# Block attention and an ELU feed-forward on one core: the second product of the last six blocks also taken as seven products of halves, transposed, with a list schedule for the work around it

## The chip, the core and the metric

The kernel runs on one core of a Trainium2 chip. Its engines work side by side, each through its own list of instructions in order: TensorE (PE in the profile, its weight loads PEld) multiplies matrices, VectorE (DVE), ScalarE (ACT) and GpSimd (POOL) do elementwise work, and SyncE (SP) issues the transfers between the chip's memory (HBM) and the core's own memory (SBUF). Matrix products land in PSUM, eight banks of 128 x 512 floats. Engines wait for each other by semaphores. The metric is the time of one execution on the device in microseconds (us).

## The reference

```python
# q, k, v: (8, 8, 576, 64) = batch, heads, tokens, head_dim
q_c, k_c, v_c = [t.reshape(B, H, 9, 64, D) for t in (q, k, v)]     # chunks of 64 tokens
scores = matmul(q_c, k_c^T) / sqrt(64);  attn = softmax(scores)    # within a chunk
x = matmul(attn, v_c) -> (4608 tokens, 512)
h = x @ w_in                                  # w_in (512, 2048)
g = where(h > 0, h, exp(min(h, 0)) - 1)
out = g @ w_out                               # w_out (2048, 512), float32
```

## The kernel before

The 4608 tokens are nine blocks of 512. x is kept transposed (features down the partitions, tokens along), so the first product gives h transposed, 128 hidden features by 512 tokens at a time (16 such rows, f = 0 to 15), and g, transposed in the same way, is the stationary operand of the second product, whose result stands in four PSUM banks o0 to o3 of 128 tokens each. Every operand of the two large products is kept as two numbers, a rounded high part and the rest (hi and lo, `ghi` and `glo`), and every product of 128x128 by 128x512 is three matmuls, hi hi + hi lo + lo hi (`three`, L400 on). ACT makes the high part, DVE or POOL the rest.

The first three blocks do this directly; the weights come in and are split in the first of them. Beside it runs the attention of a later tile of 128 tokens (`Later`): two stream transposes of q and k on DVE, 32 small matmuls for the scores, maximum and subtraction on DVE, one exponential over 128x512 on ACT, sums and normalisation on DVE, a transpose, four small transfers that swap quarters (`turned<-unturned`), and the product with v. The third block is written out by `THIRD_BLOCK`, a table of steps per f.

The last six blocks go two at a time (three rounds, `s`), and there the first product alone is made of seven products of halves (`Pair`, `PRODUCTS`): x of the two blocks and w_in are cut into 2x2 parts, sums of parts of w_in (S1 to S4) are made once and lie in HBM (`a_dram`), sums of parts of x (T1 to T4) are made by `prepare` per round, and seven products (`p1` to `p7`, six matmuls each) with kept copies and additions (`c`, `d`) give four rows of h. One pair g = 42 matmuls. The second product of the first block of the round runs in between (`Q`: three matmuls, 24 a pair), the second product of the second block stands behind all eight pairs (`KEPT`: 192 matmuls). The orders are tables written by hand (`PAIR`, `KEPT`); each letter is a step, issued on whatever engines it uses. SP loads the next operands of w_in in pieces of 256 KB in rows of 1 KB (`wi_hi<-a_dram`) and the low parts of w_out (`wo_lo<-lo_dram`, 512 KB in rows of 4 KB). Outputs of 128 tokens x 512 leave PSUM through one copy and one transfer of 256 KB in rows of 2 KB (`copy_out`).

Of the kernel before, what the change touches and what calls it, by code (L numbers as in the profile page):

```python
# [20 lines left out]
def kernel(  # L21
# [26 lines left out]
    P = 128  # L48
# [59 lines left out]

    def load_unit(u: int):
# [10 lines left out]
        if f >= 0:  # L120
            nc.sync.dma_start(
                out=st[:, len(parts)].rearrange("p a b t -> p (a b t)"),
                in_=w_out[f * P:(f + 1) * P, :],
            )
            parts.append([w.rearrange("p (a b) -> p a b", a=4) for w in w_out_slices(f)])
# [20 lines left out]
    def merge_units():  # L146
# [6 lines left out]
        for u in range(NU):  # L153
# [17 lines left out]
            for i, (hi, _) in enumerate(parts):  # L171
                nc.scalar.copy(out=hi, in_=y[:, i].bitcast(F32))
                merged.append((parts[i], y[:, i].bitcast(F32)))
# [22 lines left out]
    def load_heads(src, name: str, n0: int, pool):  # L196
        dst = pool.tile([P, H, D], F32, name=name)
# [5 lines left out]

    def load_tokens(n0: int, qk):
# [3 lines left out]
        U = 4  # L208
        for i, src in enumerate((q, k)):
            for j in range(2):  # L210
                for half in range(2):
                    w0 = i * NK * U * D + (1 - half) * Q
                    for p0, b, s0, n in pieces_of(n0, U):
                        p0 += j * D + half * Q
                        nc.sync.dma_start(
                            out=qk[p0:p0 + n // U, w0:w0 + NK * U * D].rearrange(
                                "p (h w) -> p h w", h=NK),
                            in_=src[b, j::2, s0:s0 + n, :].rearrange("h (t u) d -> t h (u d)", u=U),
                        )
# [97 lines left out]
    class Later:  # L317
# [5 lines left out]
        def load_qk(self):  # L323
            self.st = place_of_tokens(self.n)
            self.qk = load_tokens(self.n * P, self.st)
# [33 lines left out]
        def turn_a(self):  # L359
# [5 lines left out]
                op=ALU.mult)  # L365
            nc.vector.transpose(
                out=turned.rearrange("p e (j h) t -> p j h e t", j=2),
                in_=self.scores.rearrange("p j h (e k) -> p j h e k", e=2))
            nc.scalar.copy(out=unturned, in_=turned)
            for c in range(2):  # L370
# [57 lines left out]

    def elu(h, engine=nc.vector):

        e = gp.tile([P, TB], F32, name="e")
# [7 lines left out]
        ghi = gp.tile([P, TB], F32R, name="ghi")  # L439
        nc.scalar.copy(out=ghi, in_=e)  # L440
        yield
        glo = gp.tile([P, TB], F32R, name="glo")
# [3 lines left out]
    def copy_out(o, n0: int, src, on_vector: bool):  # L446

        (nc.vector.tensor_copy if on_vector else nc.scalar.copy)(out=o, in_=src)
        nc.sync.dma_start(out=out[n0:n0 + P, :], in_=o)

    def store(blk: int, o_ps):
        for tt in range(NTT):
            o = io.tile([P, DM], F32, name="q_sb" if tt % 2 else "k_sb")
            copy_out(o, blk * TB + tt * P, o_ps[tt], False)
# [609 lines left out]
```

## Time and profile before

| | |
|---|---|
| median of 3 runs | 840.24 us (840.18 to 840.9) |
| profiled execution, first to last instruction | 840.2 us |
| PE busy, granted clock | 826.3 us (98%), 0.995 of full |
| DVE, ACT, POOL busy | 501.6, 480.4, 179.0 us (60%, 57%, 21%) |
| transfers | 164.09 MB, 195 GB/s over the span |

The page gives one time for the profiled execution, its span; it stands 0.04 us below the median of the runs, so nothing of size lies around it. A row of the profile names the line of the kernel, the engine, the operation, output<-inputs, the shape, and a count; then the busy time and the mean time of one in ns. A matmul of 128x512 is listed with some 390 ns, but the next one starts before it ends, so the pace is read from chains of them. "Idle before" is time in which the engine had nothing to do, with what ended it. DMA share is the mean busy share of the 16 transfer engines.

### The profile page before, as it was taken

How to read it: one execution, taken by the hardware profiler on the slowest of the kernel's cores; microseconds unless marked ns; L12 is line 12 of the kernel's file. 1: busy time of each engine (PE TensorE's matmuls, PEld its weight loads, DVE VectorE, ACT ScalarE, POOL GpSimd, SP SyncE). 2: the span in 40 equal slices, each digit the busy share in tenths (PEclk: the TensorE clock that was granted, in tenths of full speed). 3: DMA queues.
4: the chain of work that ended last, by engine and by line, in shares of the span. 5: the costliest groups of instructions: out<-in, count | busy, mean ns of one | idle time of the engine just before them, and what ended most of it. 6: DMA issues, size and time to landing. Idle time of an engine off the chain costs nothing.

```text
span 840.2 us, 15685 instructions
## 1 busy us (share of the span) xinstructions
PE 826.3 (98%) x5949; PEld 677.0 (81%) x5949; DVE 501.6 (60%) x719; ACT 480.4 (57%) x825; POOL 179.0 (21%) x149
## 2 busy tenths in 40 slices
PE   7899999999999999999999999999999999999998
PEld 6788888887888888888888888778888888888886
DVE  4999997666775679565666746566555333233411
ACT  5999875444554547656666436655664355555521
POOL 0000014445312221111114521111126211111120
PEclk8999999999999999999999999999999999999999
DMA  9875754865787777698888656779844365545331
GB/s 240 263 228 187 247 181 152 271 205 183 232 234 218 207 193 218 191 258 239 241 240 242 191 149 200 199 233 257 238 146 138 111 198 160 164 144 163 101 101 50
DMA packets 178794, 164.09 MB, mean 195 GB/s; under 512 B 65568, under 2 KB 161312, under 8 KB 178720
## 3 DMA queue, kind: packets, MB, share of 16 engines
q1 hardware_dynamic: 178720, 163.10, 66.0%
q8 instruction: 47, 0.77, 0.4%
q14 instruction: 27, 0.22, 0.1%
HBM read 131.07 MB, written 28.31 MB: 190 GB/s over the span
## 4 chain that ended last, share of the span: by engine, by line
PE 92%; ACT 2%; DVE 2%; DMA 2%; SPq 1%; issue 1%; DVEq 0%; ACTq 0%
PE o L408 45%; PE h L408 40%; PE ps_a L235 2%; PE ps_a L243 2%; PE h L425 1%; DMA turned<-unturned 1%; SPq L199 1%; DMA k_sb<-in_k_dram 1%; PE ps_a L257 1%; PE ps_a L302 1%; SPq L373 0%; ACT st L135 0%; ACT a L280 0%; DVE e L435 0%; ACT e L433 0%
## 5 line engine op out<-in xcount | busy, mean ns | idle before, releaser
L408 PE MATMUL o<-wo_hi,ghi 128*128 128x512 f32 x416 | 163.8, 394 | 0.1
L408 PE MATMUL o<-wo_hi,glo 128*128 128x512 f32 x416 | 162.2, 390 | 0.0
L408 PE MATMUL o<-wo_lo,ghi 128*128 128x512 f32 x416 | 162.0, 390 | 0.0
L590 POOL TENSOR_TENSOR glo<-e,ghi 128x512 fp32r<-128x512 f32 x46 | 59.5, 1293 | 318.4 <-ACT ghi L588 318.4
L408 PE MATMUL h<-xhi,wi_hi 128*128 128x512 f32 x324 | 108.1, 394 | 0.0
L408 PE MATMUL h<-xlo,wi_hi 128*128 128x512 f32 x324 | 106.7, 389 | 0.0
L408 PE MATMUL o<-wo_hi,wo_lo 128*128 128x512 f32 x320 | 99.2, 389 | 0.0
L408 PEld LDWEIGHTS o<-wo_hi,ghi 128*128 128x128 f32 x416 | 78.1, 188 | 17.4 <-ACT ghi L440 0.5
L408 PEld LDWEIGHTS o<-wo_hi,glo 128*128 128x128 f32 x416 | 78.1, 188 | 16.7 <-DVE glo L443 0.4
L408 PEld LDWEIGHTS o<-wo_lo,ghi 128*128 128x128 f32 x416 | 78.1, 188 | 15.8
L629 ACT COPY kept<-h 128x512 f32<-128x512 f32 x72 | 42.2, 586 | 62.1 <-PE h L408 62.0
L408 PE MATMUL h<-wi_lo,wi_hi 128*128 128x512 f32 x288 | 75.0, 396 | 0.0
L408 PE MATMUL h<-wo_lo,wi_hi 128*128 128x512 f32 x288 | 72.9, 389 | 0.0
L408 PEld LDWEIGHTS h<-xhi,wi_hi 128*128 128x128 f32 x324 | 60.8, 188 | 12.9
L408 PEld LDWEIGHTS h<-xlo,wi_hi 128*128 128x128 f32 x324 | 60.8, 188 | 12.2
L408 PEld LDWEIGHTS o<-wo_hi,wo_lo 128*128 128x128 f32 x320 | 60.1, 188 | 12.5
L408 PE MATMUL h<-xhi,wi_lo 128*128 128x512 f32 x180 | 70.2, 390 | 0.0
L583 DVE SCALAR_TENSOR_TENSOR g_kept<-e,g_kept 128x512 f32<-128x512 f32 x48 | 33.2, 692 | 61.4 <-ACT e L580 61.4
L633 DVE TENSOR_TENSOR g_kept<-h,kept 128x512 f32<-128x512 f32 x48 | 33.1, 690 | 51.8 <-ACT kept L629 27.2
L408 PEld LDWEIGHTS h<-wo_lo,wi_hi 128*128 128x128 f32 x288 | 54.1, 188 | 11.2
L580 ACT ACTIVATE e<-e 128x512 f32<-128x512 f32 x96 | 60.7, 632 | 3.1
L408 PE MATMUL o<-wo_lo 128*128 128x512 f32 x160 | 62.2, 389 | 0.0
(114 smaller groups left out, 1330.3 us busy)
## 6 DMA issues: line engine op xcount, KB each, us to landing
wi_hi<-a_dram SPq DMA_DIRECT2D x168, 256.0 KB, 3.9
wo_lo<-lo_dram SPq DMA_DIRECT2D x52, 512.0 KB, 4.5
kept<-in_q_dram SPq DMA_DIRECT2D x100, 128.0 KB, 3.5
kept<-in_k_dram SPq DMA_DIRECT2D x100, 128.0 KB, 3.9
v_sb<-in_v_dram SPq DMA_DIRECT2D x32, 256.0 KB, 6.2
st<-in_moe_w_in_dram SPq DMA_DIRECT2D x16, 512.0 KB, 4.0
st<-in_moe_w_out_dram SPq DMA_DIRECT2D x16, 512.0 KB, 5.2
a_dram<-kept SPq DMA_DIRECT2D x16, 512.0 KB, 4.1
```

What stands on the lines that cost most here:

```text
L199: nc.sync.dma_start(out=dst[p0:p0 + n], in_=src[b, :, s0:s0 + n, :].rearrange("h s d -> s h d"))
L235: nc.tensor.matmul(scores[halves[c], j, hp, :], lhsT=qT[halves[j], hp, halves[c]], rhs=kT[halves[j], hp, halves[c]], start=True, stop=True,)
L243: nc.tensor.matmul(x_ps[halves[j], c, hp, :], lhsT=v_sb[halves[c], 2 * hp + j, :], rhs=aT[halves[c], :, j * NK + hp], start=True, stop=True,)
L257: nc.tensor.transpose(out=both[:, i, hp * P:(hp + 1) * P], in_=src[:, 2 * hp:2 * hp + 2, :], identity=ident,)
L302: nc.tensor.matmul(turned_ps[half, h, :], lhsT=a[half, h, :], rhs=ident[half, half], start=True, stop=True,)
L408: nc.tensor.matmul(ps, lhsT=a, rhs=b, start=start, stop=stop, skip_group_check=onto)
L425: nc.tensor.matmul(h, lhsT=w[:, kt, :], rhs=x[:, kt, :], start=i == 0, stop=i == len(terms) - 1)
L580: nc.scalar.activation(out=e, in_=e, func=AF.Exp, scale=-1.0)
L583: nc.vector.scalar_tensor_tensor(out=to, in0=e, scalar=-1.0, in1=c, op0=ALU.add, op1=ALU.max)
L590: engine.tensor_tensor(out=lo, in0=e, in1=hi.bitcast(F32), op=ALU.subtract)
L629: nc.scalar.copy(out=c21 if i == 4 else self.kept[i - 1], in_=x_ps)
L633: nc.vector.tensor_tensor(out=to, in0=y_ps, in1=self.kept[kept], op=ALU.add)
```

## The change

The first three blocks stay as they were, except that the 512 columns of w_out are stored in another order (`in_order`; outputs undo it on the way out), and that between the steps of the third block POOL, ACT and DVE form sums of parts of w_out (`combine_w_out`, four of eight; SP writes them to `w_dram`, and parts of w_out to `hi_dram`). The other four are made at the start of the last six blocks (`add_sums`).

In the last six blocks each round has two phases. In the first, the seven products of the first product are made for all eight g's (336 matmuls), with g of the 2x2 parts left in SBUF (`g_first`, `g_more`). In the second, the second product is made of seven products too (`SECOND`), now with w_out as the stationary operand and g as the moving one, so that the result is transposed: 7 x 8 x 6 = 336 matmuls. For it the parts of g are first subtracted and added among themselves (24 operations a round, line 1254), every one of 56 operands is split into hi and lo, and the results are added (DVE), turned back by stream transposes of DVE and sent in pieces of 64 columns (`add_out`, rows of 256 bytes). All stationary operands of both phases come through one ring of four places of 512 KB (`load_entry`), 56 loads a round.

The order is no longer a table. Every step is a job of a `Plan` with an engine, a cost in ns and the keys that it reads and writes; PE's order is fixed by the numbers given, and `Plan.order` sets jobs on ACT, DVE, POOL and SP by how soon PE needs them. Some elementwise jobs may go to DVE or POOL (`EITHER`). The exponential of a tile is made by head there: eight ACT instructions of 128x64 with the maximum as bias and the sum as a by-product, in place of a subtraction and a sum on DVE.

```diff
-    class Pair:
-    ...
-        def product(self, i: int):
-            to = y_ps if i in (2, 5, 3) else x_ps
-            (ah, al), (bh, bl) = a_operand(i), b_operand(PRODUCTS[i][1])
-            for k in range(2):
-                three(to, ah[:, k, :], al[:, k, :], bh[:, k, :], bl[:, k, :],
-                      i in (1, 2, 5) and k == 0, k == 1, onto=i not in (1, 2, 5))
-            if self.g + 1 < NS * NG:
-                load_a(self.g + 1, i)
-    PAIR = (
-        "m p1 c1 4 E Q 4 z p2 d1 Q p6 c2 h 1 Q Q 1 p5 1 q k 1 Q l p7 c3 d2 Q Q 2 p4 c4 2 Q 3 p3 d3 "
-        "3 3 3 s v x V"
-    )
+    FIRST = (1, 2, 6, 5, 7, 3, 4)
+    SECOND = (1, 2, 4, 6, 5, 7, 3)
+    PAIRS = NG // 2
+    ENTRIES = 2 * 7 * PAIRS
+    def load_entry(e: int):
+        slot, (phase, e) = ring_slot(e), divmod(e % ENTRIES, 7 * PAIRS)
+        if not phase:
+            d, o = divmod(e, 7)
+            parts = [(slot, a_dram[AOPS.index(PRODUCTS[FIRST[o]][0]), :, 2 * d:2 * d + 2])]
+        ...
+        for to, of in parts:
+            nc.sync.dma_start(out=to.bitcast(F32), in_=of)
+    def product_second(i: int, j: int, e: int, s: int, to):
+        slot = ring_slot(e)[:, j % 2].rearrange("p l (i d) -> p l i d", i=2)
+        for c in range(2):
+            three(bank(to[c]), slot[:, 0, c], slot[:, 1, c], split_place(s, 0), split_place(s, 1),
+                  i in (1, 2, 4, 5) and j == 0, j == NG - 1, onto=i not in (1, 2, 4, 5))
     ...
+    def add_softmax(t: float, n: int, begun: bool = False):
+            ...
+            def exp_by_head():
+                later[n].z = sm.tile([P, 2, NK, 1], F32, name="z")
+                for j in range(2):
+                    for h in range(NK):
+                        nc.scalar.activation(
+                            out=later[n].scores[:, j, h, :], in_=later[n].scores[:, j, h, :],
+                            func=AF.Exp, scale=SCALE, bias=mx[0][:, j, h, :],
+                            accum_out=later[n].z[:, j, h, :])
+    def add_entry(t: float, e: int):
+        count = entry_jobs(e)
+        plan.add(t, "SP", dma(count, 1320), lambda: load_entry(e),
+                 [("sums", j) for j in summed(e)], [("ring", e % 4)])
+    def add_out(t: float, s: int, h: int, c: int, sources, keys, place, place_keys):
+        ...
+        for i in range(2):
+            plan.add(t + .01 * i, "DVE", (630, 716), turn_(i), [keys[i]], [place_keys[i]])
+        plan.add(t + .05, "SP", dma(4, 2300), send, list(place_keys), [])
```

How the change moves instructions shows in three places. On PE, ahead of the profile's 624 us mark in the kernel before (second product of the second block of a round; `wo_lo` on the right side of the arrow also names the places of g's split parts, which lie in a buffer of that name), before:

```order
L408 MATMUL o_6538<-wo_hi,wo_lo 128x512
L408 MATMUL o_6538<-wo_lo 128x512
L408 MATMUL o_6538<-wo_hi,wo_lo 128x512
L408 MATMUL o_6539<-wo_hi,wo_lo 128x512
L408 MATMUL o_6539<-wo_lo 128x512
L408 MATMUL o_6539<-wo_hi,wo_lo 128x512
```

and now, in the second phase of the last round (`split`, `ghi` and `glo` are the split parts of g, `ring` a place of the ring):

```order
L434 MATMUL h<-ghi,ring 128x512
L434 MATMUL h<-split,ring 128x512 x24
L434 MATMUL o_3717<-ghi,ring 128x512
L434 MATMUL o_3717<-glo,ring 128x512
L434 MATMUL o_3717<-ghi,ring 128x512
L434 MATMUL o_3731<-ghi,ring 128x512
```

What was four banks of 128 tokens, three matmuls each, for 16 f's is now two banks at a time, six matmuls a job, for eight j's and seven products; each job waits for one split part and, every second job, for a ring place.

On SP, in the first of the last six blocks, before (one pair; `kept` from q and k is the load of a tile's tokens):

```order
L373 DMA turned<-unturned 32x256 x4
L533 DMA wi_hi<-a_dram 128x2x256
L215 DMA kept<-in_q_dram 32x4x256 x4
L215 DMA kept<-in_k_dram 32x4x256 x4
L533 DMA wi_hi<-a_dram 128x2x256 x2
L549 DMA wo_lo<-lo_dram 128x1024
L533 DMA wi_hi<-a_dram 128x2x256
L199 DMA v_sb<-in_v_dram 128x8x64
```

and now at the start of the first phase of the first round:

```order
L1599 DMA out_dram<-g_first 128x512
L598 DMA w_dram<-g_more 128x4x256 x2
L1145 DMA ring<-a_dram 128x1024 x2
L598 DMA w_dram<-g_more 128x4x256 x2
L399 DMA turned<-unturned 32x256 x4
L1145 DMA ring<-a_dram 128x1024 x2
L227 DMA kept<-in_q_dram 32x4x256
L1145 DMA ring<-a_dram 128x1024
L227 DMA kept<-in_q_dram 32x4x256 x3
L227 DMA kept<-in_k_dram 32x4x256 x3
L1145 DMA ring<-a_dram 128x1024
```

Ring loads of 512 KB stand between the same loads of tokens and, in this first phase, between the writes of the sums of w_out.

On DVE, at the end of the program, before:

```order
L448 COPY kept<-o_6813 128x512
L448 COPY kept<-o_6815 128x512
L590 TENSOR_TENSOR wo_lo<-g_kept,wo_lo 128x512 x8
L448 COPY g_kept<-o_7654 128x512
L448 COPY g_kept<-o_7656 128x512
```

and now:

```order
L1500 TENSOR_TENSOR glo<-g_more,ghi 128x512
L1251 TENSOR_TENSOR spare<-h,spare 128x512
L1251 TENSOR_TENSOR kept<-h,kept 128x512
L1251 TENSOR_TENSOR spare<-h,spare 128x512
L1251 TENSOR_TENSOR kept<-h,kept 128x512
L1411 STREAM_TRANSPOSE g_first<-spare 128x16x32 x2
L1411 STREAM_TRANSPOSE g_first<-kept 128x16x32 x2
L1251 TENSOR_TENSOR kept<-o_3717,kept 128x512
L1251 TENSOR_TENSOR kept<-o_3731,kept 128x512
L1411 STREAM_TRANSPOSE g_first<-kept 128x16x32 x2
```

Where one copy of a bank went straight to its transfer, two additions and two transposes now stand behind the last product, and four transfers of 32 partitions behind those (SP's list ends with `out_dram<-g_first`, twelve of them, after its last ring load).

More of the change, by code (lines that the diff above doesn't have):

```diff
@@ new lines, in combine_w_out @@
+    def combine_w_out():
+        for j in range(NG // 2):
+            sums = Sums(j, kept_st[2][:, :4 * TB] if j % 2 else flat(io),
+                        [w_out_slices(2 * j + i)[1] for i in range(2)])
+            sums.whole(0)
+            yield
+            sums.whole(1)
+            yield
+            sums.sum(1)
+            sums.sum(3)
+            yield
+            sums.sum(2)
+            sums.sum(4)
+            yield
+            sums.high()
+            yield
+            sums.low()
+            sums.write()
+            yield
@@ L1034, with late_tile, g_place @@
[L1034 to L1036 removed]
+    spare = late.tile([P, 2, TB], F32, name="spare")
+    kept = [kept_st[2][:, i * TB:(i + 1) * TB] for i in range(4)]
+    more = {}
+    def late_tile(key, make):
+        if key not in more:
+            more[key] = make()
+        return more[key]
+    def g_place(j: int, b: int):
+        if j < 4:
+            return g_first[:, j, b]
+        name = ("wo_hi", "wo_lo")[j // 2 - 2]
+        return late_tile(name, lambda: w0.tile([P, 2, 4, TB], F32, name="g_more", tag=name))[:, j % 2, b]
@@ new lines, in add_attention, with now, score_, v_of @@
+    def add_attention(t: float, n: int, last: int):
+        tile_n = later.get(n)
+        this = {}
+        def now():
+            return later[n]
+        if n <= last:
+            def score_():
+                later[n].score()
+            plan.add(t, "PE", (590, 800), score_, ["qT", "kT"], ["psa"])
+        before = later.get(n - 1)
+        def v_of():
+            later[n - 1].times_v()
+        def x_of():
+            later[n - 1].keep()
+        half, part = divmod((n - 1) % (2 * NTT) ^ NTT, NTT)
+        cols = "a" if part < NTT - 1 else "b"
+        plan.add(t + .01, "PE", (590, 800), v_of, ["turned", ("v", (n - 1) % 2)], ["psa"])
+        plan.add(t + .7, "ACT", ACT_PSUM, x_of, ["psa"],
+                 [(name, part) for name in (("b11", "b21") if half == 0 else ("b12", "b22"))])
+        if n <= last:
+            add_softmax(t, n)
@@ new lines, in g_more_of @@
+    def g_more_of(j: int):
+        g_place(j, 0)
+        return flat(more["wo_hi"][:, j % 2])
+    for j in range(NG // 2, NG):
+        add_sums(1 + 6 * (j - NG // 2), j)
+    for m, name in enumerate(("T3", "T4", "B22")):
+        add_prepare(.5 + .3 * m, name, "ab")
+    first_n = (PLAIN + 2) * NTT
+    later[first_n], later[first_n + 1] = attention.now, attention.following
+    add_softmax(-1.5, first_n)
+    add_turns(3.6, first_n + 1)
+    if first_n + 2 not in later:
+        add_load_qk(4.2, first_n + 2)
```

786 lines of the change are left out of this document (616 added, 170 removed), and 36 rows, old and new, of tables (KEPT, THIRD_BLOCK).

## The prediction, made blind

> **What bounds the kernel now.** I read the page's busy times and chain of waits first, then stretches of time, then the matmul chains that give PE's pace.
>
> ```profile
> span 840.2 us, 15685 instructions
> PE 826.3 (98%) x5949; PEld 677.0 (81%) x5949; DVE 501.6 (60%) x719; ACT 480.4 (57%) x825; POOL 179.0 (21%) x149
> PE 92%; ACT 2%; DVE 2%; DMA 2%; SPq 1%; issue 1%; DVEq 0%; ACTq 0%
> ```
> ```profile
> core 0: us, PE busy (x) PEld busy (x) DVE busy (x) ACT busy (x) POOL busy (x), PEclk, DMA share, GB/s
> 0.00:50.00 50.00, 41.41 (x609) 34.55 (x610) 37.06 (x62) 39.25 (x86) 0.70 (x6) 0.93 0.85 238
> 50.00:100.00 50.00, 50.00 (x396) 40.37 (x395) 47.45 (x66) 44.82 (x82) 0.00 (x0) 1.00 0.69 218
> 100.00:150.00 50.00, 50.00 (x396) 40.51 (x395) 43.76 (x61) 33.91 (x56) 12.16 (x13) 1.00 0.59 185
> 315.00:332.00 17.00, 17.00 (x135) 13.94 (x134) 15.73 (x23) 11.56 (x20) 1.05 (x1) 1.00 0.74 207
> 332.00:446.00 114.00, 114.00 (x865) 93.29 (x866) 70.29 (x113) 71.06 (x122) 19.41 (x15) 1.00 0.82 233
> ```
>
> PE is the bound: 98% busy, 92% of the chain, and 114.00 of 114.00 us in the product stage of the last six blocks, at full granted clock. DVE has 38% of that stage free (70.29 of 114); transfers do not, at a share of 0.82. So matmuls taken away shorten the run, as long as the others keep up with a shorter PE.
>
> ```profile
> 741.20 2.72 PE h L408 x12
> 756.16 2.72 PE h L408 x12
> 787.44 49.03 PE o L408 x216
> ```
> ```profile
> 398.03 1.66 PE L408 MATMUL h<-wi_lo,wi_hi 128*128 128x512 f32 x6
> 414.31 1.66 PE L408 MATMUL h<-wi_lo,wi_hi 128*128 128x512 f32 x6
> ```
>
> The first fence gives the pace: 49.03/216 = 0.227 us a matmul. It also gives a pair without attention, 756.16 - 741.20 = 14.96 us (66 matmuls); the second fence a pair with one tile's attention, 414.31 - 398.03 = 16.28. A tile's small matmuls cost PE 1.32 us.
>
> **Matmuls removed.** Per round, before: 336 for the first product and 2 x 16 x 4 x 3 = 384 for the second. Now 336 + 336. Three rounds: 144 fewer (both programs hold the same number of everything else on PE). 144 x 0.227 = **-32.7 us**. Weight loads change with them one for one and lie beside matmuls.
>
> What covered PE's neighbours before is thinner now. The next terms are what each of them needs per phase, against PE's time there: first round 348 matmuls + 5 tiles = 85.6 us, then 336 + 3 tiles = 80.2; second round 82.9 and 79.6; third 76.3 and 76.3.
>
> **DVE.** The durations:
>
> ```profile
> 413.32 0.69 DVE L633 TENSOR_TENSOR g_kept<-h,kept 128x512 f32<-128x512 f32 x1 [0.95 <-PE h L408]
> 413.93 0.68 DVE L583 SCALAR_TENSOR_TENSOR e<-e,c 128x512 f32<-128x512 f32 x1
> ```
> ```profile
> L334 DVE STREAM_TRANSPOSE qT<-kept 128x512 f32<-128x512 f32 x28 | 30.6, 1093 | 0.0
> L366 DVE STREAM_TRANSPOSE turned<-ps_a 128x512 f32<-128x512 f32 x28 | 20.1, 716 | 1.0
> L357 DVE RECIPROCAL z<-ps_a 128x8 f32<-128x8 f32 x28 | 5.8, 207 | 1.0
> L568 DVE TENSOR_TENSOR t_place<-xf,t_place 128x1024 fp32r<-128x1024 f32 x3 | 4.2, 1390 | 7.4 <-ACT t_place L567 7.3
> L573 DVE TENSOR_TENSOR xf<-xf 128x256 f32<-128x256 f32 x4 | 1.7, 423 | 0.1
> ```
>
> Two independent operations of 128x512 start 0.61 us apart (413.32, 413.93), each listed with 0.69; so 0.08 overlaps, and I take that off the others: 1.01 and 0.64 for the two kinds of transposes, 1.31 for 1024 elements, 0.98 for 768 + 256, 0.34 for 256, 0.19 for the smallest. Second phase of the first round, counted in the new order: 84 of 128x512 (51.2 us), 7 of 768 + 256 (6.9), 6 and 9 transposes (6.1 + 5.8), 3 maxima (1.8), 9 small (1.7) = 73.5. By the same count the four loaded phases are 78.5 of 85.6, 73.5 of 80.2, 63.4 of 82.9 and 69.6 of 79.6 us: 285 of 328, 87%; the third round has 42 and 56 of 76. DVE does not become the bound by its load alone. Below: nothing, since PE ran without a gap beside DVE at 47.45 of 50 (95%) and 15.73 of 17 (93%). Above: if it could not be filled past the 43.76 of 50 (87.5%) of the third row, the first two phases would take 89.7 and 84.0, together 7.9 more. It is nearest to the rows at 93 to 95%: **+3**.
>
> **ACT.** By head, an exponential takes eight pairs of rows; first and last:
>
> ```profile
> 17.18 0.31 ACT L280 ACTIVATE a<-ps_a,mx 128x64 f32<-128x64 f32 x1 [1.09 <-DVE mx L276]
> ...
> 19.41 0.24 ACT L280 ACTIVATION_READ_ACCUMULATOR a<-ps_a,mx 128x1 f32 x1
> ```
> ```profile
> 400.87 0.63 ACT L580 ACTIVATE e<-e 128x512 f32<-128x512 f32 x1
> 401.41 0.58 ACT L350 ACTIVATE ps_a<-ps_a 128x512 f32<-128x512 f32 x1
> ```
>
> 19.65 - 17.18 = 2.47 us against 0.58 (L350): 16 tiles x 1.89 = 30 us more on ACT, for some 1.2 us a tile less on DVE. At 0.54 a step (400.87 to 401.41) the fullest phase, the first, has 99 x 0.54 + 6 tiles x 2.47 + 8 casts of about 1.0 = 76 of 85.6 us. The 50-100 us row shows 44.82 of 50 with PE full, so 0.
>
> **Transfers.**
>
> ```profile
> DMA  8773955789689996899953899935999927999629
> GB/s 305 191 259 83 281 152 140 213 222 270 201 250 238 318 326 203 231 238 324 342 170 106 249 241 327 333 96 160 233 273 270 337 85 215 251 300 346 194 77 270
> q1 hardware_dynamic: 29795, 26.41, 81.1%
> wi_hi<-a_dram SPq DMA_DIRECT2D x49, 256.0 KB, 4.8
> wo_lo<-lo_dram SPq DMA_DIRECT2D x7, 512.0 KB, 6.0
> ```
> ```profile
> 399.40 0.55 SPq L199 DMA_DIRECT2D v_sb<-in_v_dram  x1
> ```
>
> The first fence is of 332 to 446 us, the second an issue of SP (0.55 us). 26.41 MB took 81.1% of 114 us, that is 92.5 us of full share, 286 GB/s; the best slices reach 346. The new first phase of round one moves 24 ring loads of 512 KB and 6 of 256, 48 + 16 token loads of 128 and 64 KB, 8 writes of sums of 512 KB, 4 outputs, and v: 28.7 MB. That is 100.4 us at 286 GB/s and 83.0 at 346, beside PE's 85.6. Bounds 0 and +14.8; nearly half of it is in rows of 4 KB instead of 1 KB, so I take the middle, **+7**. The two phases after it move 20.6 and 21.4 MB, 72 and 75 us at 286: hidden. [...]
>
> At the two borders between rounds SP stands behind four output transfers that wait for DVE; the ring holds four entries = 48 matmuls = 10.9 us. Two additions, two transposes (2.6), four issues and a landing (6.0 above) make 10.8: bounds 0 and +4 each, **+2** for both.
>
> **POOL.** In the third block POOL gets 4 x (2 + 4) sums of w_out.
>
> ```profile
> L473 POOL TENSOR_TENSOR kept<-wi_hi,wi_lo 128x512 f32<-128x512 f32 x16 | 21.3, 1350 | 157.4 <-DMA kept<-in_k_dram 117.2 <-DMA a_dram<-kept 40.1
> L473 POOL TENSOR_TENSOR kept<-kept 128x256 f32<-128x256 f32 x32 | 29.2, 932 | 1.3
> POOL glo L443 <- ACT ghi L440: 79.0, 13, 21.8
> ```
>
> 4 x (2 x 1.35 + 4 x 0.93) = 25.7 us, beside 79.0 that POOL waits there. A pair of sums (1.86) in front of a `glo` can hold up the second product: 0 to 8 x 1.86 = 14.9; most fit into the waits, **+1**.
>
> **The end.**
>
> ```profile
> 836.07 0.39 PE L408 MATMUL o<-wo_hi,wo_lo 128*128 128x512 f32 x1
> 836.50 0.69 DVE L448 COPY g_kept<-o 128x512 f32<-128x512 f32 x1 [1.96 <-PE o L408]
> out_dram<-g_kept SPq DMA_DIRECT2D x16, 256.0 KB, 2.0
> ```
>
> Now 840.2 - 836.46 = 3.7 us after PE: a copy, an issue, a landing. Then: the second addition (0.7), two transposes (0.64 + 0.72), four issues (2.2) and a landing (2.0) = 6.2, less little that overlaps = 6.0: **+2.3** (1.5 to 4).
>
> **Sum**, against the execution of 840.2 us, which is 0.04 below the median of the runs: 840.2 - 32.7 + 3 + 7 + 2 + 1 + 2.3 = **822.8 us**.
>
> **Rivals.**
>
> *All hidden (0.20).* Every neighbour keeps up: 840.2 - 32.7 + 2.3 = 809.8, to 815. For it: PE full beside DVE at 95%; against it: no stage of before had DVE, ACT and transfers all near 90% at once.
>
> *DVE's chain sets the pace (0.24), the one on the other side.* In the first two rounds additions, exponentials (ACT) and splits depend on each other, and a list in fixed order waits.
>
> ```profile
> DVE g_kept L583 <- ACT e L580: 61.4, 47, 2.4
> ```
>
> One such step waits 1.3 us. The gain left after the end is 30.4 us; it is gone when DVE's 285 us take 328 + 30.4 = 358, so when DVE is filled to 80% there. Before, it was filled to 62% in that stage, without need. At 85% these rounds take 335 us, +7; at 78%, 365, +37, and the run 847. I give 0.24 to 834 and above: 0.05 below 838.5, 0.05 within 0.2% of 840.2, 0.14 slower.
>
> *PE's clock falls in a wait (0.05).* Waits for ring places in the crowded first phase come in long pieces, and PE restarts at a lower clock. Only the first 50 us show that, at 0.93 (50 x 0.07 = 3.5 us of clock lost); all later rows above stand at 1.00. One such fall adds 3.5 to the sum: 826. [...]
>
> *The sum as worked out (0.46)*: 815 to 834. *Unnamed (0.05)*: some step that I cost at nothing; also faster for the most part.
>
> **Chances.** 0.2% is 1.7 us, about what a measurement of this kernel can tell. Faster 0.20 + 0.05 + 0.46 + 0.05 + 0.03 = 0.79; same 0.06; slower 0.15. Range 808 to 842: the low end all hidden, the high end to where the slower rival begins; outside are about 0.03 below and 0.15 above.
>
> **What would show it.** PE's matmuls of the two phases at 0.227 us, 144 fewer; idle time of PE between the start of the first round and the end of the second of 10 to 15 us, released by ring loads in the first phase and by `split` and `glo` of DVE in the second; DMA share over 0.9 in the first phase; none in the third round; about 6 us after PE's last matmul. I am wrong if PE's idle time is over 30 us (DVE or SP order), or if it stands elsewhere, in the third block above all.

## The result, and the profile after

| | before | after |
|---|---|---|
| median | 840.21 us (840.05 to 840.9) | 861.9 us (857.28 to 865.19) |
| ratio, 95% interval | | 1.0256 (1.0221 to 1.029) |
| profiled span, granted clock | 840.2 us, 0.995 | 861.4 us, 0.984 |

The change makes the kernel 2.6% slower; 822.8 us had been forecast, 808 to 842 as the range. The page of the changed kernel (busy times, chain, main queue with packets, MB and share):

```profile
span 861.4 us, 15955 instructions
PE 812.6 (94%) x5805; PEld 656.2 (76%) x5805; DVE 652.1 (76%) x998; ACT 552.0 (64%) x1143; POOL 164.5 (19%) x132
q1 hardware_dynamic: 204608, 193.51, 77.1%
PE 63%; DMA 19%; SPq 6%; ACT 5%; DVE 5%; issue 2%; DVEq 0%; ACTq 0%
```

PE lost only 13.7 us of listed busy time (826.3 to 812.6), as shorter work and a slower clock go into it together, and its share of the chain went from 92% to 63%; transfers have 19% now. Where that stands is seen by stage: the two halves of the third block, then first and second phase of each round (each from its first matmul to the next one's).

```profile
core 0: us, PE busy (x) PEld busy (x) DVE busy (x) ACT busy (x) POOL busy (x), PEclk, DMA share, GB/s
222.60:277.30 54.70, 51.38 (x449) 41.27 (x448) 34.99 (x53) 26.36 (x45) 24.29 (x23) 0.97 0.86 251
277.30:326.90 49.60, 49.42 (x450) 40.17 (x450) 37.95 (x53) 25.74 (x42) 17.63 (x14) 1.00 0.92 250
326.90:436.90 110.00, 94.49 (x670) 73.53 (x669) 85.25 (x139) 81.17 (x206) 19.42 (x13) 0.95 0.96 265
436.90:523.10 86.20, 82.41 (x530) 65.50 (x528) 78.29 (x127) 55.50 (x132) 27.51 (x14) 1.00 0.82 234
523.10:617.80 94.70, 87.31 (x657) 69.46 (x658) 62.35 (x104) 68.83 (x177) 2.55 (x2) 0.98 0.89 243
617.80:697.50 79.70, 79.70 (x498) 65.45 (x497) 73.57 (x123) 51.22 (x115) 15.53 (x7) 1.00 0.63 199
697.50:777.80 80.30, 78.13 (x337) 64.03 (x336) 45.05 (x69) 52.48 (x90) 0.00 (x0) 0.98 0.65 204
777.80:854.20 76.40, 76.19 (x336) 62.80 (x335) 56.99 (x89) 36.66 (x63) 5.84 (x4) 1.00 0.62 197
```

The same stages against PE's own work as the prediction had it, and their length in the experiments below (us; the third block took 97.9 before; * with 48 matmuls more). The first phases of rounds one and two hold five tiles each, but four each in f2, g2, j1, k1 and l1, and three and four in h1 and i1; a tile is 1.32 us of PE's work, and it moves to the second phase.

| | 3rd block | 1st, phase 1 | phase 2 | 2nd, phase 1 | phase 2 | 3rd, phase 1 | phase 2 |
|---|---|---|---|---|---|---|---|
| PE's work | 97.9 | 85.6 | 80.2 | 82.9 | 79.6 | 76.3 | 76.3 |
| after | 104.3 | 110.0 | 86.2 | 94.7 | 79.7 | 80.3 | 76.4 |
| e1 half ring | 102.8 | 100.9 | 85.8 | 86.9 | 80.3 | 76.2 | 75.9 |
| e2 whole exp | 101.6 | 108.3 | 82.5 | 95.0 | 80.3 | 77.5 | 76.0 |
| f1 both | 102.9 | 91.5 | 81.1 | 82.8 | 80.3 | 76.2 | 75.9 |
| e3 no late sums | 103.1 | 102.5 | 86.5 | 95.2 | 80.8 | 78.0 | 76.2 |
| e4 no early sums | 102.5 | 109.0 | 89.0 | 94.8 | 80.9 | 77.8 | 76.1 |
| f2 tiles spread | 105.6 | 102.2 | 85.8 | 86.9 | 81.9 | 79.2 | 76.2 |
| f3 swaps by ACT | 102.7 | 122.0 | 97.9 | 99.2 | 79.7 | 77.2 | 76.1 |
| f4 costs | 102.8 | 104.8 | 92.6 | 92.8 | 81.8 | 78.0 | 77.9 |
| g1 blocks | 104.8 | 111.5 | 82.1 | 90.8 | 80.4 | 76.4 | 76.0 |
| h1 direct first | 102.5 | 101.8 | 94.5* | 83.0 | 81.1 | 78.1 | 76.0 |
| i1 the same, no late sums | 102.9 | 96.8 | 95.1* | 81.5 | 81.0 | 78.3 | 76.1 |
| j1 spread, third row | 102.1 | 100.3 | 87.3 | 86.1 | 82.0 | 80.3 | 76.4 |
| k1 alternate | 102.1 | 95.0 | 84.3 | 87.0 | 82.6 | 78.5 | 76.9 |
| g2 blocks, spread | 105.5 | 105.3 | 86.4 | 85.3 | 81.6 | 77.3 | 76.0 |
| l1 all alternate | 104.5 | 98.9 | 84.2 | 84.8 | 82.0 | 77.5 | 77.6 |
| l2 change, alternate | 102.5 | 108.8 | 85.6 | 94.7 | 79.7 | 78.0 | 76.1 |

Each row is one execution. The third block is the same program in the rows after, e1, e2, f1, e3, f3 and f4, and took 101.6 to 104.3 there; g1, which differs from e2 only in the layout of operands in HBM and runs as long, took 3.2 more in both of the first two columns. So a difference of some 3 us between two cells doesn't show an effect by itself.

After, the losses are 6.4 + 24.4 + 6.0 + 11.8 + 0.1 + 4.0 + 0.1 us, and 3.1 at the end: 55.9, against 32.7 won on matmuls; the difference is 23.2, that of the spans 21.2. The quiet phases (the second ones of rounds two and three) run at PE's pace to 0.1 us. In the worst one, the first phase of round one, PE waited for a tile's swap, for ring places and for ACT's copies (a line gives the total in us, the number of waits, and the longest):

```profile
PE ps_a L256 <- DMA turned<-unturned: 3.6, 4, 1.6
PE o L434 <- DMA ring<-a_dram: 3.5, 2, 2.4
PE o L434 <- ACT g_first L1593: 3.4, 1, 3.4
PE o L434 <- ACT spare L1248: 2.8, 1, 2.8
PE o L434 <- ACT kept L1248: 1.5, 1, 1.5
```

The waits for transfers (ring places, and a tile's swap `turned`) are 7.1 us, those for ACT's copies 7.7. Together that is 14.8 of the 24.4 lost; falls of PE's clock, below, take up to 5.1 more in this phase, and the rest isn't assigned. The phase's transfers, by the view of that stretch (packets, MB and share; KB each and us to landing):

```profile
q1 hardware_dynamic: 24921, 29.03, 96.0%
ring<-a_dram SPq DMA_DIRECT2D x24, 512.0 KB, 6.5
```

The bytes are what the prediction counted (28.7 MB), the share is full, and the rate is 265 GB/s, not 286. A third kind of loss is PE's clock, here around one of the swaps' waits in the third block:

```profile
246.00:249.40 3.40, 1.88 (x36) 1.58 (x37) 0.20 (x1) 0.90 (x2) 1.98 (x3) 1.00 0.68 181
249.40:252.80 3.40, 3.40 (x10) 2.65 (x9) 3.14 (x7) 2.05 (x3) 0.00 (x0) 0.50 0.96 241
```

The clock stands at 0.50 for 3.41 us, 1.7 us of work lost; there are six such falls between 249 and 707 us, three of them in the first phase of round one (338, 420 and 427 us), so up to 10 us in all. The kernel before has none between its first 25 us and its last matmul.

### The profile page after: what moved, and what is told of

It reads as the page before. It is cut to its first block, busy times and chain, and to the rows that moved or that the text cites. A ratio compares the mean times of both kernels' runs of the same rounds, so it can differ in the third digit from the quotient of the medians.

```text
span 861.4 us, 15955 instructions
## 1 busy us (share of the span) xinstructions
PE 812.6 (94%) x5805; PEld 656.2 (76%) x5805; DVE 652.1 (76%) x998; ACT 552.0 (64%) x1143; POOL 164.5 (19%) x132
## 4 chain that ended last, share of the span: by engine, by line
PE 63%; DMA 19%; SPq 6%; ACT 5%; DVE 5%; issue 2%; DVEq 0%; ACTq 0%
PE o L434 33%; PE h L434 26%; DMA ring<-a_dram 7%; DMA kept<-in_k_dram 3%; DMA turned<-unturned 2%; SPq L206 1%; SPq L399 1%; PE ps_a L256 1%; SPq L227 1%; DMA ring<-w_dram 1%; DMA v_sb<-in_v_dram 1%; DMA kept<-in_q_dram 1%; DMA ring<-lo_dram 1%; PE ps_a L248 1%; DMA w_dram<-g_more 1%
## 5 line engine op out<-in xcount | busy, mean ns | idle before, releaser
L434 PE MATMUL o<-split,ring 128*128 128x512 f32 x324 | 77.2, 391 | 0.7 <-DVE split L1500 0.4
L434 PE MATMUL o<-wo_hi,ghi 128*128 128x512 f32 x192 | 77.2, 402 | 0.1
L434 PE MATMUL o<-wo_hi,glo 128*128 128x512 f32 x192 | 75.7, 395 | 0.3 <-DVE glo L479 0.3
L434 PE MATMUL o<-wo_lo,ghi 128*128 128x512 f32 x192 | 75.6, 394 | 0.0
L434 PEld LDWEIGHTS o<-split,ring 128*128 128x128 f32 x324 | 60.4, 188 | 14.3 <-DVE split L1500 0.8
L434 PE MATMUL o<-wo_lo,ring 128*128 128x512 f32 x216 | 54.6, 404 | 7.3 <-DMA ring<-a_dram 5.8
L434 PE MATMUL h<-split,ring 128*128 128x512 f32 x252 | 60.1, 390 | 0.8 <-DMA ring<-lo_dram 0.4
L434 PE MATMUL o<-wi_lo,ring 128*128 128x512 f32 x216 | 52.8, 399 | 3.4 <-ACT g_first L1593 3.4
L434 PEld LDWEIGHTS h<-split,ring 128*128 128x128 f32 x252 | 47.1, 188 | 11.4 <-DMA ring<-lo_dram 0.9
L434 PE MATMUL o<-ghi,ring 128*128 128x512 f32 x168 | 54.6, 389 | 0.0
L471 DVE SCALAR_TENSOR_TENSOR e<-e,h 128x512 f32<-128x512 f32 x48 | 32.7, 682 | 21.8 <-ACT e L469 21.6
```

Source lines behind the costliest of these rows:

```text
L434: nc.tensor.matmul(ps, lhsT=a, rhs=b, start=start, stop=stop, skip_group_check=onto)
L471: nc.vector.scalar_tensor_tensor(out=e, in0=e, scalar=-1.0, in1=h, op0=ALU.add, op1=ALU.max)
```

## Experiments: which of two causes, or both

**e1, e2, f1.** e1 halves the ring's bytes from the fifth load on, in all three rounds (it leaves out half of each operand, so its results differ from the reference); e2 gives the exponentials back to one instruction a tile; f1 has both edits.

```diff
+        if whole_e >= 4:                                             # e1, f1
+            parts = [(to[:, :1], of[:, :1]) for to, of in parts]
-    BY_HEADS = True
+    BY_HEADS = False                                                 # e2, f1
```

> From its fifth entry on, each load of the ring brings only half of its bytes (256 KB instead of 512 KB, the same number of loads in the same order; the other half of each place keeps old data, so the products are not those of the reference). Theory (transfers are the bound in the first phases of rounds one and two): the first phase of round one then moves about 17 MB instead of 29, 64 us at the 265 GB/s measured there, and is hidden; it falls from 110.0 us to 86 to 91, the second phase of round one from 86.2 to 80 to 82, the first phase of round two from 94.7 to 83 to 86, that of round three from 80.3 to 76 to 78; the run from 861 to 812 to 825, DMA share of the first phase under 0.75. Rival (the order and number of SP's issues, or ACT's copies that PE waits for): those are unchanged, so the first phase stays above 100 us and the run above 850. The third block stays at 104 us by both.

> The change without its exponentials by head: one exponential over 128x512 a tile, with subtraction and sum on DVE as before. ACT theory (eight small exponentials hold ACT 2.3 us, and PE waits for the copies of `spare`, `kept` and `g_first` behind them): those waits, about 8 us in the first phase of round one and 2 in that of round two, go, and the run falls to 848 to 853. Transfers theory: the waits on ACT there are filled by waits on transfers, the run stays within 858 to 865. DVE rival: 1.2 us a tile more on DVE, which is 92% busy in the second phase of round two, adds 3 to 10 us, mainly in second phases.

> Half the bytes of each ring load (as in the first of these runs; the products are not those of the reference) and one exponential a tile together. Halving alone left 9.1 us of waits on ACT in the first phase of round one, the whole exponential alone left 15.4 us of waits on transfers (11.6 of them for `turned`). Theory (two causes side by side, of which each hides the other when it alone is taken away): the first phase falls to 87 to 91 us (85.6 of PE's work, the rest clock), the first phase of round two to 83 to 86, the run to 820 to 827. Rival (a third cause, such as the issues of SP, which stay the same in number): the first phase stays over 95 us and the run over 832.

| | median | ratio to before |
|---|---|---|
| e1 | 840.21 | 1.0003 (0.9983 to 1.0023) |
| e2 | 855.38 | 1.0177 (1.0155 to 1.0199) |
| f1 | 823.26 | 0.9805 (0.9778 to 0.9833) |

e1 and e2 met neither theory: the runs lie between the two. (The bytes of e1 were misjudged: half of 24 loads is 6.3 MB, not 12, so 22.3 MB were left.) Their waits say why, first of e1, then of e2, both in round one's first phase:

```profile
PE o L434 <- ACT g_first L1596: 3.4, 1, 3.4
PE o L434 <- ACT spare L1251: 2.7, 1, 2.7
PE o L434 <- ACT kept L1251: 2.3, 2, 2.0
```
```profile
PE ps_a L256 <- DMA turned<-unturned: 10.3, 5, 3.7
PE o L434 <- DMA ring<-a_dram: 2.7, 3, 1.5
```

With transfers eased, PE stands for ACT; with ACT eased, it stands longer for transfers. Together the two edits take 38.6 us (861.9 - 823.3), alone 21.7 and 6.5. So 32.1 us hang on the ring's bytes once ACT is out of the way (855.4 - 823.3), and 17.0 on the exponentials by head once transfers are (840.2 - 823.3). By the table, the 32.1 stand in the first phase of round one (108.3 to 91.5, 16.8 us) and in that of round two (95.0 to 82.8, 12.2); the second phase of round one falls by 1.4 only (82.5 to 81.1), and hangs on the exponentials instead (85.8 in e1, 81.1 in f1). The theory of f1 held for the run, and for the two first phases to 0.5 us. Three stretches of f1 (columns as above), round one's two phases and round two's first:

```profile
326.00:417.50 91.50, 87.75 (x669) 70.18 (x668) 83.83 (x141) 67.69 (x118) 23.35 (x17) 1.00 0.89 249
417.50:498.60 81.10, 80.49 (x530) 65.84 (x529) 78.16 (x125) 47.72 (x85) 29.82 (x17) 1.00 0.58 161
498.60:581.30 82.70, 82.70 (x657) 67.78 (x656) 68.18 (x109) 58.60 (x105) 4.22 (x3) 1.00 0.67 183
```

The clock is whole again in all three, with no edit aimed at it: its falls went with the waits. SP's issues are as many as in the change, so their number is not the cause. DVE is at 92% in the first stretch (83.83 of 91.50) and at 96% in the second (78.16 of 81.10).

**e3, e4: the sums of w_out.** e3 leaves out the four at the start of the last six blocks, e4 the four in the third block, each with its writes (later loads bring other sums in their place; those lines are left out here).

```diff
-    for j in range(NG // 2, NG):                                     # e3
-        add_sums(1 + 6 * (j - NG // 2), j)
         elif item == "w":                                            # e4
-            next(combining_w_out, None)
+            pass
```

> The four sums of w_out at the start of the last six blocks (j = 4 to 7) are left out with their writes; loads of those sums bring the first four instead, as many bytes, so the results differ from the reference. The first phase of round one then moves 4.2 MB less. Transfers theory: 4.2 MB at 265 GB/s is 16 us, the first phase falls from 110.0 to 92 to 97 us, the run to 842 to 848. Rival (the order of SP, ACT or DVE): only the few operations of the sums go, about 10 us of DVE and POOL spread over 24 jobs; the first phase falls by less than 6 us, the run stays above 854.

> The third block without the sums of w_out (j = 0 to 3) and without the writes of sums and high parts; later loads of these bring sums of w_in instead, as many bytes, so the results differ from the reference. Theory (the sums and writes in the third block cost it 6.5 us by waits and a clock fall): the third block falls from 104.3 to 97 to 99 us, the run to 854 to 856, the phases after it unchanged. Rival (the third block is slower because of the other order of the columns of w_out or the w_in sums that were there before): it stays at 103 to 105 and the run at 861.

e3: 854.59 us (ratio 1.0137 to 1.024); the first phase fell by 7.5, between the two theories and nearer to the rival, whose run (above 854) it met: the ACT wait of 3.4 us stayed, and what was left moved at 249 GB/s. e4: 863.71 us (1.0255 to 1.0297): its theory fell. Its third block, without any of that work and at a DMA share of 0.76 and 0.62, is still 4.6 us longer than before, and within the 101.6 to 104.3 of the runs that do that work:

```profile
224.90:278.60 53.70, 49.87 (x450) 40.20 (x449) 32.68 (x51) 24.57 (x43) 6.45 (x5) 1.00 0.76 211
278.60:327.40 48.80, 48.80 (x450) 39.83 (x449) 35.48 (x50) 23.74 (x40) 10.42 (x8) 1.00 0.62 162
```

## Experiments: what the transfers are short of

All runs from here on, except l2, also contain the edit of e2 (one exponential a tile), and are compared with it.

**f2: fewer tiles in the first phase.**

```diff
-    SCORES = (9, 19, 29, 39, 49, 60, 72, 95)
+    SCORES = (9, 22, 35, 48, 60, 72, 84, 95)
-        0: "h C H e q e P l V e k S e C",
+        0: "h H e q e P l V e k S C e",
```

(The second `C` went into row 1, ahead of its two `w`.)

> One exponential a tile, the eight tiles of a round at 9, 22, 35, 48, 60, 72, 84, 95 instead of 9, 19, 29, 39, 49, 60, 72, 95 (four instead of five in the first phase, 13 steps apart instead of 10), and the last two steps of the sums of w_in in the third block one and a half rows later (`C`), behind the turning of q and k. Theory (what is late is the chain of one tile, from scores over DVE, ACT and SP's four small transfers to the product with v, which must fit between two tiles; and the third block's 5 us are those two steps ahead of q and k): waits for `turned` in the first phase fall from 11.6 to under 2 us, that phase from 108.3 to 90 to 97, the first phase of round two from 95 to 83 to 88, second phases rise by 1 to 3, the third block falls from 101.6 to 98 to 99.5; the run 822 to 833. Rival (bytes bind the phase): 28.8 MB at the 273 GB/s of that phase are 105 us, the waits move to the ring loads, and the run stays above 843.

846.18 us (1.0049 to 1.0091). The waits for `turned` went, as the theory said, and 5 us of waits for ring places and 6 for DVE stood there instead; 102.2 us for 27.7 MB are 271 GB/s at a share of 0.97, about the rival's figure (273), and the run is the rival's too. In round two, where fewer bytes move, the phase did fall to 86.9. The third block took 105.6: the moved `C` stood ahead of a split on DVE, for which PE waited 2.6 us.

**f3, f4: SP's order.** f3 issues the swaps on ACT's queue, f4 gives the plan the measured cost of transfers (the line of the ring loads is shown; token pieces, v and the writes of sums got theirs too).

```diff
-                    nc.sync.dma_start(out=turned[to, 1 - e], in_=unturned[of, e])
+                    engine.dma_start(out=turned[to, 1 - e], in_=unturned[of, e])  # f3, nc.scalar
-        plan.add(t, "SP", dma(count, 1320), lambda: load_entry(e),
+        plan.add(t, "SP", dma(count, 1900), lambda: load_entry(e),                # f4
```

> One exponential a tile, and in the last six blocks the four small transfers that swap the quarters of `turned` are issued by ACT instead of SP. Theory (they are late because they stand behind SP's other issues and behind ring loads in SP's queue): waits for `turned` fall from 11.6 to under 3 us, the first phase of round one from 108.3 to 97 to 102, the run from 855 to 842 to 848. Rival (bytes bind the phase whatever the order): waits for ring places take their place, the phase stays above 105 us and the run above 851. Second rival (ACT's four issues, 0.5 us each, delay its copies): waits on ACT of over 4 us in that phase.

> One exponential a tile, and the plan reckons with transfers as they were measured (ring load 1900 ns instead of 1320, token piece 460 instead of 400, v 920 instead of 600, sums 3700 instead of 3200), which changes SP's order. Theory (the plan believed that ring loads take 1.32 us and so put too many of them ahead of the small transfers of a tile): waits for `turned` fall below 6 us, the run to 845 to 851. Rival (bytes bind): the run stays within 2 us of 855, the waits only change their names.

Neither theory held. f3 took 888.35 us (1.0543 to 1.0605): PE no longer waited for `turned` in that phase, but 21 us for ring places. Those are the figures of the first rival (a phase above 105 us, a run above 851), but not for its reason, since the share was only 0.85: SP's own issues now waited for the swaps to land:

```profile
SPq L227 <- DMA turned<-unturned: 7.2, 5, 4.1
SPq L1145 <- DMA turned<-unturned: 6.1, 2, 3.1
SPq L598 <- DMA turned<-unturned: 5.8, 2, 4.7
```

Why an issue of a ring load waits for a swap on another queue, the trace doesn't say. f4 took 859.47 us (1.0187 to 1.0268): against e2, the first phase fell by 3.5 us and the second rose by 10.1, of which 8.3 were PE waiting for a split on DVE. Another cost in the plan moves the order in other phases too.

**g1: contiguous blocks in HBM.**

```diff
-    a_dram = dram.tile([NA, P, NG, 2, 2 * P], F32, name="a_dram")
+    a_dram = dram.tile([NA, NG // 2, P, 2, 2, 2 * P], F32, name="a_dram")
```

(`w_dram` in the same way.)

> One exponential a tile, and `a_dram` and `w_dram` laid out so that each ring load of 512 KB is one contiguous block (4 KB of each partition stand next to each other instead of 16 KB apart); same bytes, same rows of 4 KB, same order. In the crowded first phase half of the 4 KB packets took 159 ns, but their mean was 217, with single ones up to 1.7 us. Theory (the slow tail comes from rows 16 KB apart, all in the same part of HBM): the mean falls to 160 to 180, the phase moves over 300 GB/s at full share, falls from 108.3 us to 95 to 100, and the run from 855 to 838 to 846. Rival (the tail comes from many transfers at once, whatever their place): mean still over 205, phase over 105, run 852 to 858.

854.63 us (1.0141 to 1.0198), no different from e2's 855.38; the mean 4 KB packet took 207 ns instead of 217, as the rival said, and the first phase moved 266 GB/s, e2's 273. So rows that lie apart in HBM are not the cause. With the tiles spread as well, one `C` at the end of the first row and the other in the second:

> The same layout together with the eight tiles of a round at 9, 22, 35, 48, 60, 72, 84, 95, and the next to last step of the sums of w_in (`C`) at the end of the third block's first row, behind that row's last split, the last one in its second row. If the layout helps: first phase of round one 102 to 88 to 93 us, first phase of round two 87 to 83 to 85, third block 98 to 100, run 822 to 832, under the kernel before. If it doesn't: first phase 100 to 103, third block 98 to 101, run 838 to 844.

845.23 us (1.005 to 1.0099), no different from f2; the first phase (105.3) and the third block (105.5) came out longer than had been expected even for no effect (100 to 103 and 98 to 101).

**h1, i1: fewer bytes in round one.** h1 makes round one's second product directly (16 ring entries in place of 28, 64 jobs in place of 56), with three tiles in the first phase and both `C` in the third block's third row; i1 leaves out the late sums too.

```diff
+            for d in range(PAIRS):
+                for r in range(2):
+                    for m, (h, a) in enumerate(((0, 0), (0, 1), (1, 0), (1, 1))):
...
+                            three(bank(to[c]), w[:, 0, c], w[:, 1, c], split_place(slot, 0),
+                                  split_place(slot, 1), first, last)
```

> The change, but in round one alone the second product is again made directly (16 rows of hidden features, transposed as in the change, 384 matmuls instead of 336, each place of the ring used by four jobs instead of two, so 8.4 MB of ring loads in that phase instead of 14.7 and none of them sums), three tiles in round one's first phase and five in its second; one exponential a tile; the two left-over steps of the sums of w_in (`C`) back in the third block's third row. Theory (the bytes of round one bind: about 50 MB in 166 us of PE's work could not be moved at the 265 to 273 GB/s seen there): the first phase moves about 21 MB and takes 84 to 90 us (102.2 with the tiles spread, 110.0 in the change), the second 94 to 99 us (PE's work is 94), the third block 98 to 100; the run 828 to 836, faster than the kernel before in spite of 48 more matmuls. Rival (what holds up the first phase is the order of jobs on DVE, ACT and SP, whatever the bytes): the first phase stays over 97 us, and with 10.9 us of matmuls more in the second the run is 843 to 855.

> The run before (second product of round one made directly, three tiles in its first phase), without the four sums of w_out at the start of the last six blocks and their writes; later loads of those sums bring the first four, as many bytes, so the results differ from the reference. Theory (bytes alone set that phase): 27.7 MB took 101.8 us, 272 GB/s; 23.5 MB take 86 at that rate and 94 at the 250 GB/s of stretches without writes; PE's own work is 83, so the phase is 86 to 94 us, the other phases as before, the run 836 to 844. Rival (each ring place waits for something other than bytes, such as SP's order, since PE waits for ring loads alone there): the phase stays at 98 to 102 and the run over 847.

h1 took 850.6 us (1.0082 to 1.0129), i1 843.83 (1.0032 to 1.0066). First phase of h1, then of i1:

```profile
327.80:429.60 101.80, 88.95 (x541) 67.95 (x540) 73.91 (x120) 65.16 (x112) 13.80 (x12) 0.98 0.97 272
```
```profile
324.80:421.60 96.80, 86.77 (x541) 68.46 (x540) 64.24 (x102) 62.32 (x109) 4.90 (x3) 0.98 0.91 244
```

My count of h1's bytes was wrong: a tile brings 1 MB of q and k (each loaded twice over, shifted), not half of that, so 27.7 MB moved in place of 21, at 272 GB/s, about the rate of f2 (271) for as many bytes. The second phase, at a share of 0.72, came out as worked out (94.5), without a wait for the ring. The first phase of i1 lies between theory and rival, its run in the theory's range: 23.6 MB in 96.8 us, with PE waiting 6.7 us for ring places though the share is 0.91. So bytes don't set the phase to the last microsecond; a load's landing time against a ring of four places is left as a suspect. A fifth place was not tried.

**j1, k1, l1, l2: the third block again, and the order of token loads.** j1 is f2 with both `C` in the third row; k1 turns the order of the 128 KB token loads.

```diff
-        0: "h C H e q e P l V e k S e C",                            # j1
+        0: "h H e q e P l V e k S e",
-        2: "l H e q e k e e P w w",
+        2: "l H e q e k e C e C P w w",
-            load_some(n * P, later[n].st, i, piece // 2, piece % 2)  # k1
+            load_some(n * P, later[n].st, i, piece % 2, piece // 2)
```

> The change with one exponential a tile, eight tiles at 9, 22, 35, 48, 60, 72, 84, 95, and the two left-over steps of the sums of w_in (`C`) in the third block's third row instead of its first; everything else as in the change, nothing left out. Theory (those two steps, ahead of the turning of q and k on DVE and of the swaps on SP, cost the third block its first 5 us; the sums of w_out cost it nothing): the third block takes 98 to 100.5 us (104.3 in the change, 105.6 with the steps in another place of the first two rows, 97.8 in the kernel before), the run 839 to 843. Rival (the third block is slow by the writes and loads added to it, at a DMA share of 0.9): it stays at 102 to 106 with waits for `turned` in every other row, and the run at 844 to 848.

> The last run (one exponential a tile, tiles at 9, 22, 35, 48, 60, 72, 84, 95, the two left-over steps in the third row), with the token loads of q and k in another order: each brings 128 KB to 32 partitions, and neighbours in SP's list now go to partitions 0 to 31 and 64 to 95, then 32 to 63 and 96 to 127, instead of 0 to 31 and 32 to 63 first; same loads, same bytes. [...] Rival (the order of neighbours doesn't matter, since six to ten transfers are under way at once): 842 to 846, phases within 2 us.

j1: 843.85 us (1.0026 to 1.0056); the waits of 1.4 for `k_turned` and 1.7 for `turned` early in the block went, one of 1.7 for `turned` came behind the steps' new place, with a clock fall, and the block stayed at 102.1, as its rival said, within the range of the blocks that were not altered. k1: 839.93 us (0.9994 to 1.0036), below its rival's 842 to 846; the first phase fell by 5.3 us (100.3 to 95.0), where its rival allowed 2. j1's row, then k1's, same bytes:

```profile
324.40:424.70 100.30, 88.90 (x605) 69.66 (x604) 84.37 (x136) 67.37 (x116) 21.78 (x14) 0.98 0.99 277
```
```profile
325.80:420.80 95.00, 87.39 (x606) 68.27 (x605) 84.73 (x137) 67.93 (x117) 21.82 (x14) 1.00 0.97 291
```

The same edit alone in the change, and with swaps, outputs and layout in k1:

> The change as it is, with exponentials by head and its own tiles, and only the order of the token loads altered (neighbours go to partitions 64 apart). Theory (neighbouring token loads to the same part of SBUF slow all transfers): the first phase of round one falls from 110.0 us to 103 to 107, the first phase of round two from 94.7 to 90 to 93, the run from 861.9 to 851 to 857. Rival (the gain of the last run came from chance in its order): the run stays at 858 to 865.

> The last run (level with the kernel before, 839.9 us), with the four swaps of a tile and the four output transfers of a block's half put into the same alternating order, and each ring load one contiguous block of HBM; nothing left out. Theory: waits for `turned` in the third block (3.6 us) and for ring places in the later first phases (4.3 and 2.0) fall by a half, the run is 833 to 838, faster than the kernel before by 0.3 to 0.8%. Rival (these transfers are too few or too small to matter, and the layout did not matter either): 838 to 842.

l2: 857.67 us (1.0182 to 1.0241), 4.2 less than the change, but its first phase fell by 1.2 only (108.8), so neither its theory nor its rival held. l1: 839.64 (0.9972 to 1.0016), the rival's range; its first phase took 98.9, at 280 GB/s. The runs with the other order of neighbours are some 4 us shorter in both places (843.85 to 839.93, 861.9 to 857.67), but the intervals overlap, and in the first phase l1 keeps only a small part of k1's gain over j1 (100.3, 95.0, 98.9); in the later phases nothing is seen. That the order is the reason is not shown. No version that leaves nothing out beat the kernel before: k1 and l1 are level with it.

## Why the prediction was wrong

- *Matmuls, -32.7: held.* In the quiet phases PE ran at 0.227 us a matmul (76.4 us against 76.3 worked out, 79.7 against 79.6).
- *Transfers, +7, bounds 0 to +14.8: the step that failed.* With ACT out of the way (e2) that phase took 108.3 us against PE's 85.6, a loss of 22.7, clock falls included, where the term had 7, and halving the ring's bytes takes 16.8 of it away (91.5 in f1). The mechanism was right and the bytes too (29.0 MB against 28.7); the rate was not. 286 GB/s was bytes over busy share, from a stage at a share of 0.82, and there packets of 1 KB took 57 ns on average; in the last 30 us of the change's phase (406.9 to 436.9, 250 GB/s) they took 69. Two stretches of e2 show the rate itself, the first with writes of sums, the second without:

```profile
343.80:363.80 20.00, 16.89 (x129) 12.81 (x128) 17.98 (x31) 14.67 (x27) 5.87 (x5) 1.00 1.00 346
403.80:432.20 28.40, 24.63 (x158) 19.94 (x157) 19.73 (x32) 16.68 (x29) 2.58 (x2) 0.92 0.99 247
```

  By the first rate the phase's 29.03 MB would have been hidden (83.9 us against PE's 85.6), by the second they could not be (117.5). Over the whole phase the change moved 265 GB/s; that is the phase's own rate, read after the fact; the rows of before that the prediction shows have shares up to 0.85 only.
- *"The two phases after it ...: hidden": failed for the first phase of round two.* There halving the ring's bytes is worth 12.2 us (95.0 in e2, 82.8 in f1), at a mean share of 0.89 in the change. Of the second phase of round one this is not shown: it lost 6.0 us, but 3.7 of them go with the exponentials alone (82.5 in e2) and 1.4 more with the halved ring.
- *ACT, "so 0": the other step that failed, worth 6.5 us as it stands and 17 without the transfers.* The working compared loads (76 of 85.6) and did not ask what is queued behind the eight instructions. It also had them too short: 2.47 us was read at the start of the kernel before, but in the change each of the 16 tiles takes 3.44 to 3.47. The first one, and the copy that PE stood for (3.4 us, until 336.79):

```profile
332.80 0.29 ACT L1341 ACTIVATE ps_a<-ps_a,mx 128x64 f32<-128x64 f32 x1 [1.11 <-DVE mx L1326]
...
336.06 0.19 ACT L1341 ACTIVATION_READ_ACCUMULATOR ps_a<-ps_a,mx 128x1 f32 x1
336.16 0.57 ACT L1593 COPY g_first<-o 128x512 f32<-128x512 f32 x1
```

  The waits for `spare` and `kept` in that phase end in the same way, at 376.73 and 413.77 us, behind eights that end at 376.20 and 412.75. One step takes 0.44 us here and took 0.29 in the kernel before; why is not shown.
- *DVE, +3: too much.* Filled to 92% (73.57 of 79.70 in the second phase of round two), it kept PE waiting nowhere in that phase. The rival on the slower side, that DVE can be filled to 80% only, is refuted by that phase and by f1's 96%; the run was slower for another reason.
- *PE's clock falls, 0.05 for one: six.* The mechanism was on the list, as a rare one; up to 10 us hang on it, each fall behind a wait for something else.
- *POOL, +1 in the third block: the block lost 6.4, and not by the sums.* Without them (e4) it took 102.5, no less than runs that make them. PE waited there 1.9 us for `turned` and 1.4 for `k_turned`, with a clock fall behind; before, it waited for nothing. The prediction took the rest of the block as unchanged, though the table's first row now holds two steps of the w_in sums (`C`) that stood in later rows before. Moving them took away that row's waits (j1) and not the loss, so 4 to 6 us stay open. Differences that no run took out are the new order of the columns of w_out, and that `a_dram` is laid out anew, so that the sums of w_in are written to it in shorter rows: in the first half of the block the packets under 2 KB went from 11462 before to 13794 in e4.
- *SP at the borders, +2 for both: 4.3, within its bounds.* PE waited 2.1 us for a ring place at the start of round two and 2.2 in round three's first 8 us.
- *The end, +2.3: held*, 3.1: 861.4 - 854.2 = 7.2 us behind the start of the last matmul, 4.1 before.

Its own signs: PE was idle for 26.7 us from the start of round one to the end of round two (10 to 15 had been forecast, over 30 would have refuted it), and the third block, named as the wrong place, lost 6.4. With the measured losses in its sum, 840.2 - 32.7 + 55.9 = 863.4, against a span of 861.4. Even with every upper bound at once, 840.2 - 32.7 + 7.9 + 14.8 + 8 + 14.9 + 4 = 857.1, the sum stays below the result: one bound, that of the transfers, was too low, and whole terms were missing (ACT's queue, the first phase of round two, the clock falls). That f1 comes near the prediction's 822.8 is chance: its losses stand elsewhere, 5.0 us in the third block and 5.9 in the first phase.

## What to carry to other kernels

A busy share is not a capacity (in e2, stretches at a full share moved 346 and 247 GB/s): before a change adds traffic, take the rate from a stretch that is already full and has the same mix, sum the bytes of each phase, and don't call a phase hidden that is planned nearly full: here the first phase of round two, planned at 75 of 82.9 us, lost 11.8. When one operation becomes eight on an engine in fixed order, cost the wait of whatever is next in its queue (here up to 3.4 us), not only the load, and time one of the eight where it will stand (0.44 us here, 0.29 where it was read). Two causes side by side hide each other: undo them together as well as one by one, or each will seem to cost little (21.7 and 6.5 us alone here, 38.6 together).

## What the hardware showed beside that

- The clock falls came behind short waits. The largest ones just ahead of the six were 1.7, 3.4, 2.4, 1.2, 1.6 and 2.2 us, around a tile's small matmuls or a ring place; each fall lasted 3.41 us at 0.50. In the 3.41 us ahead of each fall PE was busy for 1.0 to 1.9 us. The length of a wait alone doesn't decide: one of 2.8 us, until 376.73, had no fall behind it. What does is not shown.
- In e2, stretches of 20 us with writes to HBM among the reads moved 346 and 307 GB/s at a full share, later ones of 20 and 28 us 248 and 247; without the late sums (e3), full stretches moved 262 to 268. The stretches differ in direction and in the mix of packet sizes; which of the two counts is not shown, since no run separates them. Alternating the partitions of neighbouring token loads went with 291 GB/s in k1 and 280 in l1, against 277 in j1, but with 268 against 265 in l2, so its worth is not shown.
